# Retention and an MLP on one core: a byte limit on GpSimd's loads under way, state scaling in PSUM, and transposes in other banks

One core of one Trainium2 chip. The metric is the device time of one execution in microseconds (us), lower is better. An execution's time is the span of its trace plus about 1.8 us.

## The reference

```python
# q, k, v: (8 batches, 8 heads, 576 steps, 64), float32; w_in (512, 2048), w_out (2048, 512)
scores = scale * q @ k.T                       # per head, scale = 1/8
ret    = scores * gamma[h] ** (i - j)  (i >= j, else 0)
x      = heads_side_by_side(ret @ v)           # (4608 tokens, 512)
h      = x @ w_in
out    = maximum(0.01 * h, h) @ w_out          # (4608, 512), float32
```

## The kernel before

The sequence is cut into 36 **units** of 128 tokens (two chunks of 64). For each unit: loads of k, q, v (float32, 256 KB each); casts to float16 (k on ScalarE, q and v as a product with decay factors, on VectorE up to unit 5 and on **GpSimd** from unit 6 on); a transpose of q and k (on TensorE up to unit 8, by DMA from unit 9 on, issued by SyncE); scores; masks; running states; outputs, written as x. The MLP then runs as two matmul stages, g1 (x with w_in, `hps`) and g2 (with w_out, `yps`). While the first units load, TensorE fills its time with MLP blocks of the units that are there ("the fill"); from about 80 us on it is simply full.

```python
NPE, NFIRST, NEARLY = 9, 8, 6        # first unit transposed by DMA; first steady unit; first unit cast on GpSimd
ld_pool = tile_pool(name="ld", bufs=5)
# PSUM: sc_pool (scores and states) and ot_pool (outputs), one buffer each
def load(u, x, eng):                 # cut
    eng.dma_start(out=dst, in_=src[b, :, CH*c : CH*c+n, :].rearrange("h t d -> t h d"))
def scaled(u, x, out):               # cut
    (nc.vector if u < NEARLY else nc.gpsimd).tensor_tensor(out=out, in0=t32[u, x], in1=table, op=MUL)
def cast_q(u):
    scaled(u, 0, qk16[u][:, 0])
    if u >= NPE:
        nc.sync.dma_start_transpose(out=qkT[u], in_=qk16[u])      # cut
def states(u, copy=True):            # cut: j is the chunk
    dst = a_pool.tile([P, NP, CH], FP, name="stmp") if ends_block else s32[:, j]
    nc.vector.tensor_tensor(out=dst, in0=st[:, j], in1=prev, op=ADD)            # st is in PSUM
    if ends_block:
        nc.vector.tensor_tensor(out=s32[:, j], in0=dst, in1=gblk, op=MUL)       # "the scaling"
# GpSimd issues, in this order: q and v of unit 0, units 1, 2, 3, w_in 0..3 (two halves each),
# w_out 0, unit 4, w_out 1, unit 5, w_out 2, w_out 3, units 6, 7, 8; then, with the rest of the fill:
some(8, 9); scores(5); masks(5); states(5)
loads(9, nc.gpsimd)
casts(6)
some(9, 12)
loads(10, nc.gpsimd)
casts(7)
some(12, 13)
outputs(5)
some(13, 14)
transposes(6, sc_pool)
...
loads(11, nc.gpsimd); casts(8)
...
transposes(7, sc_pool); outputs(6); loads(12, nc.sync); casts(9); loads(13, nc.sync) ... casts(10); loads(14, nc.sync)
```

GpSimd both issues these loads and does the casts of units 6 on, strictly in this order; and `dst = stmp` makes the scaling read two SBUF operands.

## Time and profile before

| | before |
|---|---|
| time, median of 4 runs | 311.13 us (307.52 to 313.3) |
| span of the profiled run | 311.8 us |
| TensorE busy | 295.0 us (95%) |
| GpSimd busy | 118.0 us (38%) |
| mean granted TensorE clock of that run | 0.989 |

Two more lines of the page of the kernel before, which the prediction does not quote: what the DMA engines moved in 40 slices of 7.8 us, and the chain that ended last. Then two rows of its DMA view, for the weight loads (KB each, then the median us from issue to landing).

```profile
GB/s 197 242 200 226 212 263 238 278 186 147 249 198 245 229 224 168 187 194 157 182 164 176 175 166 154 187 171 171 175 67 80 75 84 36 36 34 36 34 69 67
...
PE 91%; DVE 4%; issue 1%; DMA 1%; ACT 1%; POOL 0%; POOLq 0%; ACTq 0%
...
w_in<-in_moe_w_in_dram POOLq DMA_DIRECT2D x8, 256.0 KB, 10.5
w_out<-in_moe_w_out_dram POOLq DMA_DIRECT2D x4, 512.0 KB, 9.0
```

The path to the end is nearly all TensorE. A w_in transfer is under way for 10.5 us because several stand behind each other; the engines move over 200 GB/s meanwhile.

From TensorE's timeline of the kernel before (start, us, what, count): the transposes of unit 6, and the scores of unit 11, a milestone. From unit 11's scores to the end it takes 311.8 - 88.8 = 223.0 us.

```profile
55.28 0.61 PE L184 MATMUL sc<-ident,qk 128*128 128x128 f16 x8
...
88.78 0.32 PE L203 MATMUL sc<-qkT 64*64 64x64 f16 x16
```

### The profile page before, as it was taken

Reading aid. Unit: us, or ns where it says so; the run is one execution under the profiler, and the core shown is the slowest. Engines: PE = TensorE matmul, PEld = TensorE weight load, DVE = VectorE, ACT = ScalarE, POOL = GpSimd, SP = SyncE. Lnnn points to the kernel's source line nnn. Section 1 sums busy time; section 2 is a strip of 40 time slices with the busy share of each in tenths; the row PEclk is TensorE's granted clock in tenths of the full one; section 3 lists DMA queues with packets and bytes.
Section 4 is the critical chain, followed back from the end, with each engine's and each line's share of the span. In section 5 each row is a group of like instructions: output and inputs, shape, how many; then the busy total and the mean of one; then the engine's idle time right before and its main releaser. Section 6 shows DMA issues by size and latency. Waiting matters only on the chain.

```text
span 311.8 us, 9364 instructions
## 1 busy us (share of the span) xinstructions
PE 295.0 (95%) x4120; PEld 199.3 (64%) x4120; DVE 112.0 (36%) x210; ACT 140.2 (45%) x242; POOL 118.0 (38%) x142
## 2 busy tenths in 40 slices
PE   2769999989999999999999999999999999999995
PEld 1547854665766666666666666666666666666663
DVE  2840133644543334333434333333333334332001
ACT  4635733555654444444444444444444444343320
POOL 8934949940645241514142423333333330000000
PEclk9998999979999999999999999999999999999999
DMA  7899998978999996876796767776713230000011
GB/s 197 242 200 226 212 263 238 278 186 147 249 198 245 229 224 168 187 194 157 182 164 176 175 166 154 187 171 171 175 67 80 75 84 36 36 34 36 34 69 67
DMA packets 117368, 49.73 MB, mean 160 GB/s; under 512 B 106128, under 2 KB 110608, under 8 KB 117328
## 3 DMA queue, kind: packets, MB, share of 16 engines
q1 hardware_dynamic: 109760, 35.60, 48.9%
q0 software_dynamic: 7136, 13.37, 18.5%
q8 instruction: 32, 0.52, 0.7%
q10 hardware_dynamic: 432, 0.17, 0.3%
q14 instruction: 8, 0.07, 0.1%
HBM read 36.81 MB, written 9.44 MB: 148 GB/s over the span
## 4 chain that ended last, share of the span: by engine, by line
PE 91%; DVE 4%; issue 1%; DMA 1%; ACT 1%; POOL 0%; POOLq 0%; ACTq 0%
PE hps L425 40%; PE yps L448 35%; PE sc L203 3%; PE hps L493 2%; PE yps L493 2%; PE sc L212 2%; PE ot L305 2%; PE ot L316 1%; DMA t<-in_q_dram 1%; DVE s L245 1%; PE yps L638 1%; DVE s L221 1%; PE yps L184 1%; PE hps L361 1%; PE sc L184 1%
## 5 line engine op out<-in xcount | busy, mean ns | idle before, releaser
L425 PE MATMUL hps<-xT,w_in 128*128 128x256 f16 x1152 | 148.7, 276 | 0.0
L432 ACT ACTIVATE gt<-hps 128x512 f16<-128x512 f32 x144 | 86.0, 597 | 129.1 <-PE hps L425 128.9
L425 PEld LDWEIGHTS <-w_in 128*128 128x128 f16 x1152 | 113.4, 99 | 39.5 <-issue 0.3
L448 PE MATMUL yps<-w_out,gt 128*128 128x512 f16 x496 | 126.6, 380 | 0.0
L254 POOL CAST st<-s 128x512 f16<-128x512 f32 x28 | 17.1, 610 | 144.8 <-DVE s L243 69.9
L448 PEld LDWEIGHTS <-gt 128*128 128x128 f16 x496 | 46.2, 98 | 33.9
L328 DVE TENSOR_TENSOR xT<-ot,own 128x512 f16<-128x512 f32 x32 | 22.1, 692 | 78.2 <-ACT own L324 78.2
L458 DVE COPY osb<-yps 128x512 f32<-128x512 f32 x31 | 21.2, 685 | 73.9 <-PE yps L448 73.9
L147 POOL TENSOR_TENSOR v<-t,cs 128x512 f16<-128x512 f32 x30 | 31.5, 1049 | 0.0
L147 POOL TENSOR_TENSOR qk<-t,cs 128x512 f16<-128x512 f32 x30 | 31.3, 1043 | 0.1
L221 DVE TENSOR_TENSOR s<-sc,cs 128x512 f16<-128x512 f32 x36 | 24.6, 684 | 11.3 <-PE sc L212 11.3
L144 ACT CAST qk<-t 128x512 f16<-128x512 f32 x36 | 22.2, 620 | 1.0 <-DMA t<-in_k_dram 1.0
L324 ACT COPY own<-ot 128x512 f32<-128x512 f32 x32 | 18.7, 586 | 7.7 <-PE ot L316 5.9
L243 DVE TENSOR_TENSOR s<-sc,s 128x256 f32<-128x256 f32 x40 | 16.8, 420 | 0.7
L203 PEld LDWEIGHTS <-qkT 64*64 64x64 f16 x576 | 8.1, 111 | 10.8 <-issue 8.0
L212 PE MATMUL sc<-v,qk 64*64 64x64 f16 x576 | 11.4, 198 | 2.2 <-issue 2.2
L184 PEld LDWEIGHTS <-qk 128*128 128x128 f16 x72 | 5.7, 118 | 11.7 <-ACT qk L144 4.9
L203 PE MATMUL sc<-qkT 64*64 64x64 f16 x576 | 11.9, 203 | 1.2 <-ACT qkT L190 0.9
L134 POOL DMA_DIRECT2D t<-in_q_dram x13 | 11.4, 875 | 4.3 <-DMA t<-in_k_dram 2.2
L134 POOL DMA_DIRECT2D t<-in_k_dram x12 | 10.4, 870 | 6.4 <-DMA t<-in_k_dram 2.4
L134 POOL DMA_DIRECT2D t<-in_v_dram x13 | 11.2, 863 | 1.2 <-DMA w_in<-in_moe_w_in_dram 1.1
L184 PE MATMUL yps<-ident,qk 128*128 128x128 f16 x32 | 4.5, 309 | 7.1 <-ACT qk L144 4.8
(43 smaller groups left out, 148.8 us busy)
## 6 DMA issues: line engine op xcount, KB each, us to landing
out_dram<-osb SPq DMA_DIRECT2D x35, 256.0 KB, 2.3
t<-in_k_dram SPq DMA_DIRECT2D x22, 256.0 KB, 3.5
t<-in_q_dram SPq DMA_DIRECT2D x21, 256.0 KB, 4.1
t<-in_v_dram SPq DMA_DIRECT2D x21, 256.0 KB, 4.3
t<-in_q_dram POOLq DMA_DIRECT2D x11, 256.0 KB, 4.8
t<-in_v_dram POOLq DMA_DIRECT2D x11, 256.0 KB, 5.0
t<-in_k_dram POOLq DMA_DIRECT2D x10, 256.0 KB, 4.9
w_in<-in_moe_w_in_dram POOLq DMA_DIRECT2D x8, 256.0 KB, 10.5
```

The source lines that it names most:

```text
L134: eng.dma_start(out=dst, in_=src[b, :, CH * c : CH * c + n, :].rearrange("h t d -> t h d"))
L144: nc.scalar.copy(out=qk16[u][:, 1], in_=t32[u, 1])
L147: (nc.vector if u < NEARLY else nc.gpsimd).tensor_tensor(out=out, in0=t32[u, x], in1=tab_sb[:, kind(u), x // 2, :].unsqueeze(2).to_broadca ...
L203: nc.tensor.matmul(out=a[half(j), g, 0, p, :], lhsT=qkT[u][half(g), 1, p, half(j)], rhs=qkT[u][half(g), 0, p, half(j)], start=True, stop=T ...
L212: nc.tensor.matmul(out=a[half(g), j, 1, p, :], lhsT=qk16[u][half(j), 1, 2 * p + g, :], rhs=v16[u][half(j), 2 * p + g, :], start=True, stop ...
L221: nc.vector.tensor_tensor(out=s16s[u], in0=sc_tiles[u][:, :, 0], in1=mask_sb.unsqueeze(1).unsqueeze(1).to_broadcast([P, 2, NP, CH]), op=MUL,)
L324: nc.scalar.copy(out=tmp.rearrange("q c (j t) -> q c j t", t=CH), in_=own.rearrange("q j c t -> q c j t"),)
L328: nc.vector.tensor_tensor(out=xT[:, :, t0 : t0 + P].rearrange("q (s g) t -> q g s t", g=2), in0=far, in1=tmp.rearrange("q (s g) t -> q g s ...
L425: nc.tensor.matmul(out=hps[:, f, :], lhsT=w_in16[:, c, fc * P : (fc + 1) * P], rhs=xT[:, c, t0 % XR : t0 % XR + tok], start=(c == 0), stop ...
L432: nc.scalar.activation(out=g_tiles[g][:, fb * nf : (fb + 1) * nf, :], in_=hps, func=mybir.ActivationFunctionType.Lrelu,)
L448: nc.tensor.matmul(out=y_cur[g, tb], lhsT=g_tiles[g][:, f, tb * P : (tb + 1) * P], rhs=w_out16[:, f, :], start=(f == 0), stop=(f == NF - 1),)
L458: nc.vector.tensor_copy(out=osb, in_=y_cur[g, tb])
```

## The change

Its intent: keep at most 1.75 MB of GpSimd's loads under way, so that other DMA work, such as instruction fetches, doesn't stand behind them; scale a block-end state out of PSUM, so that the scaling doesn't contend with GpSimd for SBUF; and put three units' transposes in the output banks, so that they needn't wait for the state arithmetic. The ring is kept in software: before a load that would exceed the limit, GpSimd copies one element of the oldest load's destination ("the probe"), which makes it wait until that has landed.

```diff
+    RING = 7 << 18
+    landing = []
+    probe = const_pool.tile([P, P], FP, name="probe")
+    def ring(size, at):
+        while landing and sum(n for n, _ in landing) + size > RING:
+            x = landing.pop(0)[1]
+            nc.gpsimd.tensor_copy(out=probe[0:1, 0:1], in_=x)
+        landing.append((size, at))
 ... in load(), for GpSimd alone:
+            if eng is nc.gpsimd:
+                ring(H * n * D * 4, dst[0:1, 0, 0:1])
 ... in load_w_in(), for each half (0.5 MB):
+            ring(CH * NP * FQ * 4, w_in16[CH * o : CH * o + 1, 0, fs.start : fs.start + 1])
 ... in load_w_out() (1 MB):
+        ring(P * 4 * DM * 4, w_out16[0:1, 4 * c, 0:1])
 ... in transposes():
-            both = pool.tile([P, 2, 2 * NP, P], F16, name="sc")
+            both = pool.tile([P, 2, 2 * NP, P], F16, name="sc" if pool is sc_pool else "ot")
 ... in states():
-            dst = a_pool.tile([P, NP, CH], FP, name="stmp") if ends_block else s32[:, j]
+            dst = st[:, j] if ends_block else s32[:, j]
 ... in the order of the fill: transposes(5 / 7 / 8, sc_pool) become transposes(5 / 7 / 8, ot_pool),
     units 5 and 7 one block earlier, unit 8 three
```

More of the change, by code (lines that the diff above doesn't have):

```diff
@@ L583 @@
     states(4)
-    some(5, 6)
-    transposes(5, sc_pool)
-    some(6, 8)
+    transposes(5, ot_pool)
+    some(5, 8)
     outputs(4)
@@ L609 @@
     state_copy(6)
-    more(g1[2], 3, 4)
-    transposes(7, sc_pool)
-    more(g1[2], 4, 5)
+    transposes(7, ot_pool)
+    more(g1[2], 3, 5)
     outputs(6)
@@ L622 @@
     state_copy(7)
+    transposes(8, ot_pool)
     casts(10)
@@ L626 @@
     outputs(7)
-    more(g2, 2, 3)
-    transposes(8, sc_pool)
-    more(g2, 3, 5)
+    more(g2, 2, 5)
     run(ends[4], g1_blocks(3), g2[5:])
```

## The prediction

> **What bounds the kernel now.** I read four views in this order: busy time by slices, the waits of TensorE, the timeline of its first 80 us, then the timelines of VectorE and GpSimd beside it. The page says TensorE sets the end:
>
> ```profile
> PE   2769999989999999999999999999999999999995
> POOL 8934949940645241514142423333333330000000
> PEclk9998999979999999999999999999999999999999
> DMA  7899998978999996876796767776713230000011
> ```
>
> From slice 10 on (after 78 us) TensorE is full at full clock; the order of matmuls there is untouched by the change, except for one waiting copy. So whatever is won or lost lies before 80 us, in the fill. There TensorE idles for these reasons:
>
> ```profile
> PE yps L184 <- ACT qk L144: 4.8, 2, 4.5
> PE yps L184 <- DVE qk L147: 2.3, 2, 1.3
> PE sc L212 <- issue: 2.2, 1, 2.2
> PE sc L184 <- DVE s L243: 2.0, 1, 2.0
> ```
>
> The first two are the first loads and stay. The third is at 19.41 us. The trace holds one 16 KB packet of the instruction queue at 19.43 us, 0.94 us long, and TensorE resumes at 21.65: it waited for its own instructions. The clock records then give half clock from 22.8 to 26.2 us. Half speed for 3.4 us is 1.7 us lost, so this stall costs 2.2 + 1.7 = **3.9 us**. The fourth comes from this stretch of VectorE:
>
> ```profile
> 59.54 0.41 DVE L243 TENSOR_TENSOR stmp<-sc,s 128x256 f32<-128x256 f32 x1
> 59.98 3.12 DVE L245 TENSOR_TENSOR s<-stmp,cs 128x256 f32<-128x256 f32 x1
> 63.14 0.42 DVE L243 TENSOR_TENSOR s<-sc,s 128x256 f32<-128x256 f32 x1
> ```
>
> The scaling of a block-end state, elsewhere 0.42 us, took 3.12 us while GpSimd ran its casts back to back (59.77 to 66.0 us). TensorE's transposes of unit 7 needed that bank and began 2.0 us late, at 63.62; half clock followed from 63.8 to 67.2, again 1.7 us: **3.7 us**. Were both gone and nothing else in the way, 312.4 - 7.6 = 304.8 us.
>
> What could be in the way is GpSimd, which issues the loads of units 6 to 11 and casts those units in the same order of program:
>
> ```profile
> 34.22 1.53 POOL L345 DMA_DIRECT2D w_out<-in_moe_w_out_dram  x2
> 35.71 0.94 POOL L134 DMA_DIRECT2D t<-in_k_dram  x1
> ...
> 49.44 0.88 POOL L134 DMA_DIRECT2D t<-in_v_dram  x1
> 50.42 1.06 POOL L147 TENSOR_TENSOR qk<-t,cs 128x512 f16<-128x512 f32 x1
> ```
>
> The cast of unit 6's q ends at 51.5 us. TensorE's transposes of unit 6 start at 55.28, so there is **3.8 us of slack**, just what the instruction stall costs.
>
> **What the Trainium skill says.** "SBUF — State Buffer", section "Who interferes with whom": a VectorE instruction with two SBUF inputs contends with a GpSimd instruction that reads SBUF, one with at most one SBUF input outside the two-port modes does not. The trace agrees: L245 reads two SBUF tiles and was 3.12 us once against 0.42; L243, with one input from PSUM, has a mean of 420 ns in both its forms. "DMA: Bandwidth & Descriptors", section "Issuing engines are not separate DMA queues": all issuers share 16 DMA engines. The trace's packet records fit that the instruction fetch stands behind load data: fetches follow each other about every 256 instructions, and by that spacing the one at 19.43 should have been asked for near 12 us; 8 transfers were then under way. "TensorE: Matmul & The Clock Gate", Part 1, puts the gate's window near 3.4 us and the cold clock at half; both cold windows here are 3.4 us at 0.5.
>
> **The change, part by part.** *States in PSUM.* 16 additions write to PSUM in place of SBUF, and 16 multiplications read one PSUM and one SBUF input. Counts stay; each should be 0.42 us as the other PSUM forms (the 16 of L245 have a mean of 594 ns now). On the path only the one at 59.98 counts: 3.12 - 0.42 = 2.7 us, which covers the 2.0 us wait, and the cold window with it.
>
> *Transposes in the output banks.* The same 8 matmuls and two copies for each of units 5, 7 and 8, a block or so earlier, waiting for the copy out of the output bank in place of the state arithmetic. It removes 0.5 us (unit 5 on L240) and backs up the former part. No work is added.
>
> *The ring.* 40 one-element copies are put on GpSimd (147 to 187 rows in the built order). Its smallest instruction now, a 128x1 memset, is 0.10 us, so about 4 us of work, spread out. What they wait for costs more. A 256 KB tile counts 0.25 MB, a w_in transfer 0.5 and a w_out transfer 1 (float32 source). Hence from the order of the changed kernel: w_out 0 waits until the seventh w_in has landed, w_out 1 for w_out 0, w_out 2 for w_out 1, w_out 3 for **all** before it including w_out 2, k of unit 7 for w_out 3, and v of unit 9, after which come unit 6's casts, for q of unit 7. Before, only a count of 8 held them.
>
> Landings now, from the trace: seventh w_in 26.9, w_out 31.1, 35.4, 42.3, 45.0 us. A lone tile (k of unit 10, issued at 52.41, landed at 56.10) needs 3.7 us, of which 0.88 is the issue and 0.75 its data (the spacing of landings at 44 to 48 us), so about 2 us is latency. A w_out behind an empty queue then needs 0.77 issue + 2 + 2.7 data (spacing of w_out 2 and 3) = 5.5 us, plus 0.3 for wait and probe. This gives w_out 0 at about 32, w_out 1 at 37.5 (the tiles of unit 4 fill part of the gap), w_out 2 at 43.5, w_out 3 at 43.5 + 5.8 = 49.3. Then k7, q7, v7, k8 issue without a wait (4 x 0.88 = 3.5), and q8, v8, k9, q9, v9 with a probe each (5 x 1.1 = 5.5): unit 6's casts start at 49.6 + 9.0 = **58.6 us in place of 50.4**, and its q is ready near 59.7, or 57.5 if the DMA engines lag less on w_out than they do now (their slowest is 1.3 to 3 us behind the fastest there).
>
> TensorE, freed of the instruction stall, would want it at 55.3 - 3.9 = 51.4. It waits some 7 to 8 us and starts unit 6 near 59: 3.7 us later than now, whether or not the stall goes. Such an idle time, longer than the 2.2 us that cooled the clock before, makes one cold window: 1.7 us. Later casts do not bind: unit 7's q is ready about 59.7 + 1 + 3 x 1.1 + 1 = 65, and TensorE, with 5.2 us of work and 1.7 us cold between transposes 6 and 7, arrives at 66; unit 8's q (70) has still more room. Sum: + 3.7 (unit 6 late) + 1.7 (cold) - 3.7 (the stall on L245 and its cold window) = +1.7, with perhaps 1 us given back by the earlier transposes of units 7 and 8 and by small waits there: **+0.7, so 313.1 us**.
>
> **The rivals.** *A, the ring costs nothing:* the instruction fetch comes in time, loads keep up, both stalls go. For it: the two stalls are real, a run at 307.5 among 313.3 and 312.4 looks as if one of them can be absent, and 1.75 MB is 5 us of data at the 0.35 MB/us seen, more than the 3.7 us that a tile is under way. Against: w_out 3 and k7 cannot overlap with what they wait for. It would give 305 to 306. *B, the ring holds GpSimd longer than I reckon,* each probe nearer 0.4 us and each landing set by the slowest DMA engine: unit 6 at 62, with units 7 and 8 late too and a second cold window; 316 to 319. *C, the fetch stall stays and the casts are only 3 us late:* unit 6 at 58; then the stall costs nothing further, because TensorE would wait for GpSimd anyway; 311 to 312.
>
> **Range and chances.** The sum and C lie within 2 us of the time before; I weigh them about 0.7, A or a part of it 0.2, B 0.1. The kernel before itself spread over 6 us. Predicted 313.0 us, 8 in 10 between 307.0 and 317.0. Faster by over 2% needs less than 306.2, all of A: 0.14. Slower by over 2% needs more than 318.7: 0.05. Within: 0.81.
>
> **What would show it.** *States:* the scaling at 0.42 us everywhere, no long one near 60 us, no wait of L184 on the state arithmetic. *Fetch:* no "issue" wait near 19 us, and no cold window at 23 to 26; if it is shorter but there, the fetch still stands behind loads. *Ring:* GpSimd idle on w_out and tile landings between 27 and 50 us, its first cast at 57 to 60, and a new TensorE wait of 4 to 8 us on GpSimd's qk of unit 6, followed by half clock. If that cast begins before 53 us, the step on landings is wrong, and A holds. If the wait is there and the time still is below 306, then what I reckon as lost after it is made up elsewhere in the fill, since from 80 us on nothing can be.

## The result, and the profile after

| | before | after |
|---|---|---|
| median (runs) | 311.13 us (4) | 322.55 us (4; 321.08 to 323.53) |
| profiled run: time, span | 313.62, 311.8 us | 321.08, 319.3 us |
| TensorE busy | 295.0 us | 293.7 us |
| mean granted clock, profiled run | 0.989 | 0.989 |

The ratio is 1.0446, 95% interval 1.0342 to 1.0549: **4.5% slower**. Here and below a ratio is the mean time of one kernel's fast runs over that of the other's of the same rounds, and a run over 1.5% above the fastest of its kernel is counted as slow and left out. All four runs of the changed kernel were fast. Of the kernel before, only 307.52 and 309.83 can have been counted: 312.43 and 313.3 are over that limit, and 322.43 / 1.0446 gives the mean of the other two. The medians, which take in all runs, differ by 3.7%. The changed kernel's 322.55 us lies above the range predicted, 307 to 317 us.

The page of the changed kernel (line numbers have shifted: transposes are L197, casts L160, probes L132, g1 L440, the scaling L258):

```profile
PE   2789797189999999999999999999999999999995
...
POOL 8935745999264333333333424252525240000000
PEclk9999999879999999999999999999999999999999
...
GB/s 200 235 131 121 196 191 151 262 235 260 196 231 194 208 182 206 207 189 245 188 150 192 179 176 163 190 179 171 161 102 35 101 59 76 33 35 35 33 65 68
...
PE 75%; DMA 10%; POOL 7%; issue 4%; DVE 1%; ACT 1%; POOLq 0%; ACTq 0%
```

TensorE has a hole in slice 7 (56 to 64 us) that wasn't there, and slices 2 and 3 (16 to 32 us, the w_in stage) move 131 and 121 GB/s in place of 200 and 226. The path to the end now runs over DMA and GpSimd for 17%. TensorE's waits:

```profile
PE sc L197 <- POOL qk L160: 7.7, 1, 7.7
...
PE yps L508 <- DMA w_out<-in_moe_w_out_dram: 2.3, 2, 2.1
...
PE hps L440 <- ACT gt L447: 1.7, 1, 1.7
PE hps L440 <- DMA w_in<-in_moe_w_in_dram: 1.6, 2, 1.1
```

The wait on "issue" near 19 us and the 2.0 us on the state arithmetic are gone, as intended; 7.7 us on GpSimd's cast of unit 6 and the three smaller entries, all from late loads, have come (the 1.7 us on ScalarE too: its activation stood behind its cast of k of unit 4, which waited 1.6 us for the load). GpSimd's timeline shows why that cast is late (in brackets the idle time before, and what ended it):

```profile
29.07 0.17 POOL L132 CAST probe<-w_in 1x1 f32<-1x1 f16 x1 [1.73 <-DMA w_in<-in_moe_w_in_dram]
29.53 0.76 POOL L360 DMA_DIRECT2D w_out<-in_moe_w_out_dram  x1 [0.28 <-issue]
...
48.56 0.17 POOL L132 CAST probe<-w_out 1x1 f32<-1x1 f16 x1 [3.59 <-DMA w_out<-in_moe_w_out_dram]
...
54.73 0.17 POOL L132 CAST probe<-w_out 1x1 f32<-1x1 f16 x1 [2.30 <-DMA w_out<-in_moe_w_out_dram]
...
58.70 0.17 POOL L132 COPY probe<-t 1x1 f32<-1x1 f32 x1
58.82 0.88 POOL L147 DMA_DIRECT2D t<-in_q_dram  x1
...
63.78 1.05 POOL L160 TENSOR_TENSOR qk<-t,cs 128x512 f16<-128x512 f32 x1
```

Before, the first cast began at 50.42 us. Now GpSimd sits in probes until each w_out has landed, one w_out after the other, then issues nine loads, then casts. The answering lines of TensorE's timeline, which again end with the milestone, 319.3 - 96.3 = 223.0 us before the end:

```profile
64.90 0.61 PE L197 MATMUL sc<-ident,qk 128*128 128x128 f16 x4 [7.65 <-POOL qk L160]
...
96.27 0.32 PE L216 MATMUL sc<-qkT 64*64 64x64 f16 x16
```

So all the difference of the two traces lies before unit 11's scores: 96.27 - 88.78 = 7.5 us, the whole of 319.3 - 311.8. (In 12 of the 15 kernels' traces it takes 223.0 to 223.2 us from there to the end; e3 needs 223.8 and e10 and e13 224.6, with a wait or a spell of half clock behind the milestone.) Unit 6 starts 64.90 - 55.28 = 9.6 us later; from there to the milestone the changed kernel needs 31.4 us in place of 33.5, because the wait on the scaling has gone:

```profile
70.40 0.43 DVE L256 TENSOR_TENSOR sc<-sc,s 128x256 f32<-128x256 f32 x1
70.87 0.42 DVE L258 TENSOR_TENSOR s<-sc,cs 128x256 f32<-128x256 f32 x1
```

That is not yet the work of the state part: GpSimd's cast before this scaling ends as it begins (69.83 + 1.05 = 70.88 us), and in e2 below, with the ring alone, the old scaling takes 0.42 us too.

**Traces and medians.** The medians differ by 11.4 us, the traces by 7.5. The two profiled executions are one draw each: that of before (313.62, itself over the limit of 1.5%) is 2.5 us over its median, that of after (321.08) 1.5 us under its own, which makes up the 3.9 us. The mean clock of a run says how many cold windows it had (stretches of 3.4 us at half of TensorE's clock): one takes 0.0055 off a mean over 310 us. In 55 runs of the kernel before, 44 had a mean of 0.998 or more, that is no cold window, ten had one and one had two. The trace that I read had two (0.989). The spread that remains is not explained here: the 44 runs without a cold window took 305.5 to 312.1 us.

### The profile page after: what moved, and what is told of

It reads as the page before. It is cut to its first block, busy times and chain, and to the rows that moved or that the text cites. A ratio compares the mean times of both kernels' runs of the same rounds, so it can differ in the third digit from the quotient of the medians.

```text
span 319.3 us, 9428 instructions
## 1 busy us (share of the span) xinstructions
PE 293.7 (92%) x4120; PEld 198.6 (62%) x4120; DVE 110.2 (35%) x210; ACT 139.8 (44%) x242; POOL 126.6 (40%) x185
## 3 DMA queue, kind: packets, MB, share of 16 engines
q1 hardware_dynamic: 109760, 35.60, 50.1%
q0 software_dynamic: 7136, 13.37, 19.0%
## 4 chain that ended last, share of the span: by engine, by line
PE 75%; DMA 10%; POOL 7%; issue 4%; DVE 1%; ACT 1%; POOLq 0%; ACTq 0%
PE hps L440 34%; PE yps L463 33%; DMA w_in<-in_moe_w_in_dram 5%; POOL t L147 4%; DMA w_out<-in_moe_w_out_dram 4%; PE sc L216 2%; DMA t<-in_k_dram 2%; POOL probe L132 1%; PE ot L329 1%; PE ot L318 1%; PE sc L225 1%; PE yps L650 1%; PE hps L508 1%; POOL w_out L360 0%; DVE s L234 0%
## 5 line engine op out<-in xcount | busy, mean ns | idle before, releaser
L440 PE MATMUL hps<-xT,w_in 128*128 128x256 f16 x1152 | 146.3, 273 | 3.2 <-ACT gt L447 1.7
L440 PEld LDWEIGHTS <-w_in 128*128 128x128 f16 x1152 | 112.1, 98 | 41.7 <-issue 3.2
L463 PEld LDWEIGHTS <-gt 128*128 128x128 f16 x496 | 46.2, 98 | 34.1
L160 POOL TENSOR_TENSOR qk<-t,cs 128x512 f16<-128x512 f32 x30 | 31.3, 1043 | 0.1
L160 POOL TENSOR_TENSOR v<-t,cs 128x512 f16<-128x512 f32 x30 | 31.2, 1042 | 0.0
L197 PEld LDWEIGHTS <-qk 128*128 128x128 f16 x72 | 5.6, 117 | 16.3 <-POOL qk L160 7.8
L508 PEld LDWEIGHTS <-gt 128*128 128x128 f16 x64 | 6.3, 103 | 9.4 <-issue 4.1
L160 DVE TENSOR_TENSOR qk<-t,cs 128x512 f16<-128x512 f32 x6 | 4.1, 688 | 20.9 <-DMA t<-in_q_dram 20.9
```

The lines of the kernel that those rows point to most:

```text
L440: nc.tensor.matmul(out=hps[:, f, :], lhsT=w_in16[:, c, fc * P : (fc + 1) * P], rhs=xT[:, c, t0 % XR : t0 % XR + tok], start=(c == 0), stop ...
L463: nc.tensor.matmul(out=y_cur[g, tb], lhsT=g_tiles[g][:, f, tb * P : (tb + 1) * P], rhs=w_out16[:, f, :], start=(f == 0), stop=(f == NF - 1),)
```

## The experiments

Thirteen kernels, in four groups, each group on one chip; every one was correct, and each was traced in one execution. The rival explanations at the start: the ring's waiting, the probes' own work, the state part, the bank part.

### Which part of the change it is

**e1_no_ring**: the changed kernel with `RING = 1 << 40`, so that no probe is ever made.

```diff
-    RING = 7 << 18
+    RING = 1 << 40
```

> The changed kernel with the ring's limit set so high that it never acts and no probe is built; states in PSUM and the transposes in the output banks stay. Theory (the ring alone makes the kernel slow, by holding GpSimd until loads have landed): as fast as the kernel before or up to 3.7 us faster, 307 to 311 us, unit 6's casts again near 50 to 51 us, no 3.1 us scaling on VectorE, no wait of L197/L184 on the state arithmetic. Rival (the transposes moved into the output banks hold TensorE or the copies): it stays above 316 us.

**e2_ring_only**: the kernel before plus the ring, neither of the other two parts.

```diff
+    RING = 7 << 18   (and landing, probe, ring() and its three calls, as in the change)
```

> The kernel before with the ring alone added (1.75 MB). Theory: 320 to 327 us, GpSimd's first cast at 62 to 65 us, TensorE waits 6 to 9 us on GpSimd's q of unit 6; the instruction wait near 19 us absent. Rival (transposes at fault): 308 to 313 us.

**e3_states_only**: the kernel before plus

```diff
-            dst = a_pool.tile([P, NP, CH], FP, name="stmp") if ends_block else s32[:, j]
+            dst = st[:, j] if ends_block else s32[:, j]
```

> The kernel before with only the block-end states scaled in PSUM. Theory: the one long scaling (3.12 us) becomes 0.42 us, the 2.0 us wait of unit 7's transposes and the half clock after it go: 306.5 to 310 us where the run before shows both. Rival (the wait has another cause, or GpSimd delays the PSUM form too): same as before within 1 us, with a wait of 1.5 us or more still ahead of unit 7's transposes.

**e4_ot_only**: the changed kernel without ring and with the old `dst` line, so that only the transposes of units 5, 7 and 8 have moved.

```diff
-    RING = 7 << 18
+    RING = 1 << 40
-            dst = st[:, j] if ends_block else s32[:, j]
+            dst = a_pool.tile([P, NP, CH], FP, name="stmp") if ends_block else s32[:, j]
```

> The kernel before with only the transposes of units 5, 7 and 8 moved into the output banks. Theory: they no longer wait for the state arithmetic, so the 2.0 us wait ahead of unit 7 goes too, though the long scaling of 3.1 us on VectorE stays and holds up the copies behind it (the copy of unit 7's q and the sum of unit 6's outputs), so part of the wait may come back at scores of unit 7: 307 to 311 us. Rival: slower than before by 2 us or more, because the bank is freed later.

| same chip, before 310.57 us (7 runs) | median | ratio, 95% interval | first GpSimd cast |
|---|---|---|---|
| e1_no_ring | 309.16 | 0.998 (0.992 to 1.005) | 48.7 us |
| e2_ring_only | 322.76 | 1.041 (1.033 to 1.048) | 65.5 us |
| e3_states_only | 308.72 | 0.996 (0.987 to 1.004) | 49.2 us |
| e4_ot_only | 311.76 | 1.004 (0.996 to 1.012) | 50.1 us |

The ring alone makes the whole loss, and without it nothing is lost. (In e2 the first cast came later than the 62 to 65 us expected, and a wait for instructions of 0.9 us was left.) The state part does what it is for, but e3 doesn't show it: no cast ran beside the scaling there. e1 does. Its scaling lay wholly beside GpSimd's casts, took 0.42 us, and nothing waited for it; e5, e6 and e7 have the same. VectorE's line of e1, then GpSimd's:

```profile
58.70 0.42 DVE L258 TENSOR_TENSOR s<-sc,cs 128x256 f32<-128x256 f32 x1
```

```profile
58.08 1.06 POOL L160 TENSOR_TENSOR qk<-t,cs 128x512 f16<-128x512 f32 x1
59.08 1.05 POOL L160 TENSOR_TENSOR v<-t,cs 128x512 f16<-128x512 f32 x1
```

The bank part alone doesn't do what it is for: in e4 VectorE's timeline has the long scaling again, and TensorE's wait of 2.0 us is still there, now of the outputs on a copy behind that scaling.

```profile
60.33 2.46 DVE L258 TENSOR_TENSOR s<-stmp,cs 128x256 f32<-128x256 f32 x1
```

```profile
PE ot L318 <- DVE qkT L203: 2.0, 1, 2.0
```

"SBUF — State Buffer", section "Who interferes with whom", which the prediction cites, agrees with e4 and e1: the scaling with two SBUF inputs took 2.46 us beside GpSimd's casts, with one of them in PSUM 0.42 us.

### What in the ring it is

Three theories: the probes' instructions; the waiting on landings; and of this, w_in or w_out.

**e5_probes_free**: the same probes at the same places, but reading a constant that is long there, so they wait for nothing.

```diff
-            x = landing.pop(0)[1]
-            nc.gpsimd.tensor_copy(out=probe[0:1, 0:1], in_=x)
+            landing.pop(0)
+            nc.gpsimd.tensor_copy(out=probe[0:1, 0:1], in_=cs[0:1, 0:1])
```

> The changed kernel with all 40 probes kept in their places, but each reads a constant that landed at the start, so that none waits for a load; the loads are again held only by the count of 8. Theory (the waiting costs, not the instructions): GpSimd's first cast near 51 to 54 us, time 308 to 312 us. Rival (the probes themselves take GpSimd's time): first cast after 58 us, time above 316 us.

**e6_ring_early**: the ring for GpSimd's first 15 loads only (11 tiles of q, k, v and half of w_in).

```diff
     def ring(size, at):
+        issued.append(size)                  # issued = [] stands before
+        if len(issued) > 15:
+            return
```

> The changed kernel with the ring in force for the first 15 of GpSimd's transfers only (up to the second part of w_in), 12 probes in place of 40. Theory: the first instruction fetch comes before 16 us as with the whole ring, so no instruction wait near 19 us in any run, while the w_out loads overlap again: first cast at 50 to 53 us, wait of the transposes of unit 6 below 2 us, time 305.5 to 308.5 us and little spread. Rival (the early part of the ring is what costs): above 315 us.

**e7_ring_3mb**: the same ring with a limit of 3 MB.

```diff
-    RING = 7 << 18
+    RING = 12 << 18
```

> The changed kernel with a limit of 3 MB in place of 1.75. Theory: no w_out transfer waits for the one before it any more, so first cast at 51 to 55 us, 307 to 312 us; the instruction wait may be back in some runs. Rival (any such limit costs through probes and their waits): above 316 us.

**e8_wout_small**: a w_out load counted as 0.25 MB in place of 1, so that the w_outs hardly wait for each other.

```diff
-        ring(P * 4 * DM * 4, w_out16[0:1, 4 * c, 0:1])
+        ring(P * 4 * DM, w_out16[0:1, 4 * c, 0:1])
```

> The changed kernel with the limit of 1.75 MB, but a w_out transfer counted as 0.25 MB in place of 1, so that w_out transfers no longer wait for one another; the w_in part is held as in the change. It tells how the loss divides between w_in and w_out. By the landings of the changed kernel, w_in cost about 2 us and the four w_out about 8 more: first cast at 54 to 57 us, TensorE waits 1 to 4 us there, time 309 to 315 us. Were w_in the larger part: above 317 us.

| same chip, before 310.58 us (55 runs) | median (runs) | ratio, 95% interval | first GpSimd cast | TensorE's wait for unit 6 |
|---|---|---|---|---|
| e5_probes_free | 309.51 (20) | 1.004 (1.001 to 1.007) | 51.1 us | none |
| e6_ring_early | 309.02 (20) | 1.002 (0.999 to 1.005) | 50.3 us | none |
| e7_ring_3mb | 308.58 (20) | 0.996 (0.993 to 1.000) | 50.1 us | 0.5 us |
| e8_wout_small | 315.09 (4) | 1.015 (1.001 to 1.029) | 57.8 us | 4.0 us |

In this group the ratios lean against the new kernels: 30 of the 55 runs of the kernel before are over 1.5% above the fastest (305.53 us) and so left out, but one at most of each new kernel's. Over all runs the medians of e5, e6 and e7 are 0.3%, 0.5% and 0.6% under the kernel before; e6 missed the 305.5 to 308.5 us expected of it.

The probes' work is nearly free; their waiting costs. At 3 MB there is hardly any. In e8 some 40% of the loss is left (315.1 against 309.2 without the ring and 322.6 with it; the record's verdict on e8 is unclear, as its interval holds 2%), though the w_outs no longer wait for each other. Of GpSimd's delay of 7.4 us against the kernel before, 5.0 are there when w_out 0 lands (36.1 against 31.1 us), so they come from the w_in stage; later a probe also waits 2.0 us for w_out 3, before unit 8's loads. The last landing of each load (the slowest DMA engine's) shows the delay adding up:

| us | 7th w_in | w_out 0 | w_out 1 | w_out 2 | w_out 3 | first cast |
|---|---|---|---|---|---|---|
| before | 26.8 | 31.1 | 35.4 | 42.3 | 44.9 | 50.4 |
| predicted for after | 26.9 | 32 | 37.5 | 43.5 | 49.3 | 58.6 |
| after | 28.95 | 35.3 | 41.4 | 48.4 | 54.6 | 63.8 |
| e8_wout_small | 28.4 | 36.1 | 40.9 | 47.5 | 51.0 | 57.8 |
| e7_ring_3mb | 25.3 | 29.5 | 34.4 | 41.9 | 44.5 | 50.1 |

### How it reaches TensorE

The trace says: TensorE waits for unit 6's cast, which stands on GpSimd behind held loads, while unit 6's q had landed at 56.1 us. If that wait were the cost, moving the casts should win it back. The rival: more than that one cast is late.

**e9_vector_casts**: units 6 to 8 cast on VectorE.

```diff
-    NEARLY = 6
+    NEARLY = 9
```

> The changed kernel, with the casts of units 6, 7 and 8 given to VectorE (NEARLY = 9): GpSimd still issues the loads one behind the other under the same ring, so the data come as late as in the changed kernel, but no cast stands behind them in GpSimd's order. Theory (the ring reaches TensorE because GpSimd's casts stand behind the held loads; the data of unit 6 are there long before): q of unit 6 is issued at about 50.6 us and landed by 55, VectorE is idle from 52.3 to 55.7 us in the changed kernel, so unit 6's q is cast by 56 to 57, TensorE's 7.7 us wait for it goes (0 to 1 us left), no half clock from 60 to 68, and the time falls by 7 to 9 us to 313 to 316 us. The wait for w_out of 2 us stays. Rival (the data themselves, or the DMA engines, are too late, whoever casts): a wait of 4 us or more for unit 6's q on DVE in place of POOL, and 319 us or more.

**e10_casts_first**: unit 6's casts ahead of unit 9's loads.

```diff
-    loads(9, nc.gpsimd)
     casts(6)
+    loads(9, nc.gpsimd)
```

> The changed kernel, with the casts of unit 6 one place earlier in GpSimd's order: before the loads of unit 9 rather than after them. The loads of unit 9 take three probes and three issues, 0.88 + 0.17 us each with gaps, 3.1 us in all. Theory (order on GpSimd passes the delay on, microsecond by microsecond): the first cast begins near 60.7 us in place of 63.8, TensorE's wait for it is 4.4 to 4.8 us in place of 7.7, and the time is 2.5 to 3.5 us under the changed kernel's 322.5: 319 to 320. Rival (unit 6 is late because of the data, or the end is set by something else in the fill): the wait and the time stay, 322 to 323.

Same chip, before 310.79 us (20 runs): e9 **321.44 us**, ratio 1.034 (1.028 to 1.039); e10 **322.55 us**, ratio 1.034 (1.028 to 1.041). My theory foretold the waits and not the time. In e10 the first cast began at 62.4 us rather than 60.7, and the wait for unit 6 did fall from 7.7 to 4.7 us, but the time did not move. TensorE's timeline of e10 has a new wait at the milestone, for the transposes of unit 11:

```profile
98.66 0.33 PE L216 MATMUL sc<-qkT 64*64 64x64 f16 x16 [2.43 <-DMA qkT<-qk]
```

(That execution was the slowest of its four, 325.12 us, with half clock from 98.8 to 102.2 us after this wait.) In e9 the wait for unit 6 is gone altogether, and other waits stand in its place; TensorE's waits in e9:

```profile
PE hps L440 <- DVE xT L341: 3.7, 1, 3.7
PE sc L216 <- DMA qkT<-qk: 3.3, 2, 2.7
...
PE yps L508 <- DMA w_out<-in_moe_w_out_dram: 1.9, 1, 1.9
```

On VectorE the addition that makes unit 5's output stood behind unit 7's casts, and these waited for their load (VectorE's timeline of e9):

```profile
60.30 0.69 DVE L160 TENSOR_TENSOR qk<-t,cs 128x512 f16<-128x512 f32 x1 [2.36 <-DMA t<-in_q_dram]
...
62.47 0.68 DVE L341 TENSOR_TENSOR xT<-ot,own 128x512 f16<-128x512 f32 x1
```

Further on, the transposes by DMA of units 10 and 11 came late. The second kind comes from supply, not from where unit 6 is cast; the first from late loads together with the order on VectorE that e9 itself made. So two more kernels, one for each open question: is a late GpSimd enough without any held load; and what sets the end once e9's first new wait is taken away?

**e12_late_gpsimd**: no ring; twelve products of the size of a cast put before unit 6's casts.

```diff
-    RING = 7 << 18
+    RING = 1 << 40
     loads(9, nc.gpsimd)
+    filler = const_pool.tile([P, H, D], F16, name="filler")
+    for _ in range(12):
+        nc.gpsimd.tensor_tensor(out=filler, in0=idle, in1=table, op=MUL)   # cut
     casts(6)
```

> The changed kernel without the ring (as in the run without the ring), but GpSimd does twelve more products of the size of a cast between the loads of unit 9 and the casts of unit 6: it is late by about 12 x 1.04 = 12.5 us from there on, as late as under the ring, while w_in, w_out and the data of units 4 to 9 come as early as without the ring. Theory (GpSimd's lateness from unit 6's casts on is enough by itself): first cast of unit 6 near 61 us, TensorE waits 6 to 8 us for it, half clock after it, and 317 to 321 us against 309 without the ring. Rival (the loss needs the late loads of w_in and w_out and the underfed DMA engines as well): 314 us or less.

**e13_vector_reordered**: e9 with unit 7's casts moved.

```diff
     loads(10, nc.gpsimd)
-    casts(7)
     some(12, 13)
     outputs(5)
     some(13, 14)
     transposes(6, sc_pool)
+    casts(7)
```

> The kernel with the casts of units 6 to 8 on VectorE (e9, 321.4 us), with unit 7's casts put after unit 5's output addition and unit 6's transposes in program order, so that VectorE's addition no longer stands behind data that lands at 60 us. Theory (the whole supply under the ring is late, and the next gate behind is the transposes by DMA of unit 11, issued by SyncE at 91.4 us behind earlier loads): the 3.7 us wait for the addition goes, the waits for those transposes grow from 3.3 to 5 us or more, unit 11's scores still start at 94 to 96 us, and the time is 318.5 to 322 us. Rival (my own order on VectorE was what kept e9 slow): both kinds of wait together fall under 4 us, and the time is 314 to 317 us.

Same chip, before 311.21 us (7 runs): e12 **320.82 us**, ratio 1.037 (1.028 to 1.047); e13 **321.63 us**, ratio 1.039 (1.026 to 1.051). (Three of the seven runs of the kernel before are left out as slow, and the record's verdict on both is "unclear" though the intervals lie above 2%; by the medians they are 3.1% and 3.3% slower.) e12 has w_in, w_out and the data up to unit 9 as early as without the ring; GpSimd's loads of units 10 and 11 come after the fillers and are late too. It loses about what the ring loses: TensorE's waits there and the cast's start (48.07 + 13.37 = 61.4 us, the fillers being one row) come out as expected. The waits of e12:

```profile
PE sc L197 <- POOL qk L160: 7.6, 1, 7.6
```

So a GpSimd that is 12 us late at unit 6 is **sufficient** for the loss. e13 shows that the wait for unit 6 is not the only gate. The 3.7 us wait is gone there, and unit 11's scores start when they did in e9, because its transposes are no earlier. TensorE's timelines of e9 and e13, each with two lines:

```profile
86.74 0.32 PE L216 MATMUL sc<-qkT 64*64 64x64 f16 x16 [0.55 <-DMA qkT<-qk]
...
95.60 0.32 PE L216 MATMUL sc<-qkT 64*64 64x64 f16 x16 [2.71 <-DMA qkT<-qk]
```

```profile
86.60 0.32 PE L216 MATMUL sc<-qkT 64*64 64x64 f16 x16 [1.30 <-DMA qkT<-qk]
...
95.59 0.34 PE L216 MATMUL sc<-qkT 64*64 64x64 f16 x16 [2.83 <-DMA qkT<-qk]
```

Unit 11's scores at 95.6 us plus the fixed 223 us give the end of e9 (318.8) to 0.2 us; e13's 320.2 has one more cold window (95.8 to 99.2 us, 1.7 us). In the changed kernel they start at 96.27, without a wait, but their transposes had landed only at 95.69: this gate stood 0.6 us behind, hidden by the wait for unit 6. Its place varies: in e2 and e10 the scores wait for it until 98.65 and 98.66 us, in e12 the transposes land at 93.35, before TensorE wants them. My figure for the transposes' wait in e13 was too high (5 us or more; 4.1 measured), since TensorE had lost 2.2 us to ScalarE and 3.2 to w_out on the way. The milestone, 94 to 96 us, and the time were as expected.

What holds that gate is seen in part. SyncE issues unit 11's transposes at 91.44 us in e9, 91.72 in e13 and 90.94 in the changed kernel, against 82.49 before, in one queue behind the transposes of units 9 and 10 and the loads of units 13 to 15; the first of these transposes, unit 9's, starts at 72 to 77 us as against 68, behind GpSimd's late casts. From the one to the other that queue took 14.0 us in the changed kernel, no longer than before (14.5), so its lateness was there from unit 9's cast on. Why it took 19.5 us in e9 is open: the first transpose's issue alone was 6.1 us long.

### A version from the best parts

**e11_states_3mb**: the kernel before, with the `dst` line of e3 and the ring of e2 at 3 MB.

```diff
+    RING = 12 << 18   (and the ring as in the change)
-            dst = a_pool.tile([P, NP, CH], FP, name="stmp") if ends_block else s32[:, j]
+            dst = st[:, j] if ends_block else s32[:, j]
```

> The best parts together: the kernel before, with block-end states scaled in PSUM and a ring of 3 MB; the transposes stay in the banks that they had. Theory: the wait on the 3 us scaling is gone, the ring seldom waits, and w_in is held enough that the instruction fetch comes in time: a profile near 305 us, first GpSimd cast near 50 us, and a median of 306.5 to 309 us against some 311 before (ratio 0.985 to 0.995). Rival (the transposes in the output banks were what made the 3 MB run good, or the gain is only in the profile): ratio 0.997 to 1.003.

308.97 us (15 runs) against 310.79 (20 runs): ratio 0.995 (0.992 to 0.998). It is better than the kernel before by 0.5%, at the edge of what was expected (0.985 to 0.995), and no better than e7 or e3 as far as these intervals tell. Its profile still has 0.6 us of TensorE waiting for instructions.

## Why the prediction was wrong, point by point

- **Mechanism: right.** GpSimd's first cast late behind probes, a new wait of TensorE on that cast, half clock after it: all there. The direction was hardly forecast: +0.7 us is inside the noise, and I gave 0.14 to faster by 2% and 0.05 to slower. That the wait measured 7.65 us, as forecast (7 to 8), is luck: its start and its end were both 5.9 us later than I had them. Rival B, the ring holding GpSimd longer, "unit 6 at 62 ... 316 to 319", is in its first half what happened, and more than so: 64.9. I gave it 0.1. Its waits for units 7 and 8 did not come.
- **The step that failed: the landings under the ring**, "w_out 0 at about 32, w_out 1 at 37.5, w_out 2 at 43.5, w_out 3 at 43.5 + 5.8 = 49.3 ... unit 6's casts start at 49.6 + 9.0 = 58.6". Measured: 35.3, 41.4, 48.4, 54.6 and 63.8. My own sum was short as well: 5.8 us four times from 26.9 gives 50.1, not 49.3. I took the seventh w_in at 26.9 from the old trace, as though the ring left the w_in stage alone; it landed at 28.95, 2.05 us of the error. From it to the first w_out took 6.34 us rather than 5.1, and the next three 6.1, 7.0 and 6.2 rather than 5.5, 6.0 and 5.8: 3.3 us. Issue and probes after the last w_out, the 9.0 us, were right (63.78 - 54.73 = 9.05). The probes were 43 in the trace, not 40, at 0.17 us or more, and GpSimd's busy time rose by 8.6 us (118.0 to 126.6), not 4; e5 shows that this hardly counts.
- **The sum.** Predicted: unit 6 late + 3.7, cold + 1.7, the scaling's stall - 3.7, given back - 1. Measured in the traces: unit 6 late **+ 9.6**, cold + 1.4 (2.8 us of work at half clock, 64.9 to 67.7 us), the scaling's stall - 3.7 (2.0 and 1.7; in e2 the ring alone removes it), together 7.3 of the 7.5 us. The first term carries the whole error of the traces' difference: 5.2 us of late landings, 0.7 because I rounded the cast's end down.
- **"TensorE ... would want it at 51.4."** It wanted it at 57.25: it had lost 1.6 us to w_in, 1.7 to ScalarE and 2.3 to w_out. I had no term for those. They cost nothing further where the cast is awaited anyway, but they are why taking away that wait could not have won 7.7 us.
- **A step that I left out: the gate behind.** "Later casts do not bind" held for units 7 and 8, and I stopped there. Unit 11's transposes by DMA landed 0.6 us before they were wanted in the changed kernel; units 10 and 11 bind in e9 and e13.
- **The trace I started from** had two cold windows, and 44 of 55 runs have none. My gain of 1.7 us for each was in that trace, not in the median; hence 11.4 us in the medians against 7.5 in the traces, and the smallness of what e1, e3, e7 and e11 win.
- **States:** 0.42 us everywhere, as expected. **Fetch:** the trace's first packet of the instruction queue came at 14.4 us in place of 19.4, and the wait on it went. The other traces show that the ring brings it forward: 14.4 to 16.6 us in the seven with w_in, or in e6 half of it, held at 1.75 MB (the changed kernel, e2, e6, e8, e9, e10, e13), 17.0 to 19.4 in the six with no load held (before, e1, e3, e4, e5, e12), 16.0 and 18.5 at 3 MB. The wait does not follow so simply: e2 (0.9 us) and e11 (0.6 us) still have one and e3, without a ring, has none. What it could win is small: e6 and e7, which carry the other two parts as well, gain at most 0.7% (e7's interval; 0.6% by its median).

## What to carry to other kernels

Leave room in a limit on bytes under way for what moves during a round trip: here 1.75 MB serialised 1 MB transfers that each took some 6 us to come back, 3 MB didn't. If the engine that enforces the limit also does other work in order, all of that work, not only the loads, is late by every wait. Before you claim the longest wait as the prize, find the next gate behind it, and take several executions' clock and time, not one trace, as the base. Where a ratio leaves runs out, look how many of each kernel.

## What the Trainium skill lacked or had wrong

- "DMA: Bandwidth & Descriptors", section "Anatomy of one DMA — SWDGE (gpsimd) path", gives 2.0 us plus bytes over 436 GB/s, an estimate of 4.4 us for a 1 MB read. With only three later tiles beside it, w_out 3 took 5.6 us from its issue (49.02) to its last landing (54.61), and w_out 2, behind three tiles, 6.4 us (42.02 to 48.44). The page's own table under "Bandwidth", with 6.15 us of DMA time for 1 MB, is nearer. No run here has a 1 MB load alone, so the fit is not shown wrong for that.
- The same section calls descriptor generation "small, variable". For loads issued by GpSimd the traces show the issue holding that engine for 0.88 us for each 256 KB tile and 0.61 to 0.77 us for a weight load, and 0.28 us of nothing before each weight load that follows a probe of a weight: nine tile loads are 8 us during which GpSimd casts nothing. The page's row on first-byte latency, about 1 us for "the Q7 emission overhead", is nearer.
- No page says what an element-sized copy used as a wait costs: 0.17 us on GpSimd where the load has landed, and otherwise a wait for the last of the load's 16 engines, which for the seventh w_in came 0.6 us after the next (28.36 and 28.95), for w_out 2 0.7 us (47.78 and 48.44).
